# One step of a search or of its places behind a piece of the experts' products, and a later first penalty

## The chip, the cores and the metric

The kernel runs on one core of one Trainium2 chip. Its engines are TensorE (PE, with PEld for its weight loads), VectorE (DVE), ScalarE (ACT), GpSimd (POOL) and SyncE (SP, which only issues transfers here). The metric is the device's time for one execution, in microseconds: the median of several runs.

## What is computed

Two parts, one behind the other. The first is a convolution along the sequence by way of a Fourier transform; the second sends each of its 19968 rows to one of eight experts.

```python
X = np.fft.rfft(x, axis=1)                      # x: 8 x 2496 x 256
y = np.fft.irfft(X * (filt_r + 1j * filt_i), n=2496, axis=1)
...
logits = x @ w_gate                             # x = y as 19968 x 256, eight experts
order = np.argsort(-logits.flatten())
for idx in order:                               # greedy, best logit first
    tok, e = idx // E, idx % E
    if assigned[tok] >= 0 or counts[e] >= cap:  # cap = 19968 / 8 = 2496
        continue
    assigned[tok] = e
    counts[e] += 1
...
for e in range(E):                              # w1: 8 x 256 x 1024, w2: 8 x 1024 x 256
    out[assigned == e] = np.maximum(x[assigned == e] @ w1[e], 0) @ w2[e]
```

So every expert gets exactly 2496 rows, and who gets which is settled by a greedy pass over all logits.

## The kernel before

The first 420 us are the transform, its inverse, the logits (`lg`, 117 x 176 x 8) and the first search. The rows go to `xs` in device memory.

The greedy pass is done without a sort. It falls into eight phases; each finds, by a search, the threshold at which the next expert fills up, and which expert that is (`Route.phase`). A search has eleven rounds (`threshold`). In a round VectorE compares the best logit of each token with up to nine thresholds (`Gm`, L587); TensorE multiplies the mask with the one-hot experts `A` (eleven short matmuls, L595); VectorE folds the counts (`t`, `D`, `X`, L603 to L605); TensorE sums them over the partitions (L608); and VectorE takes the next three bits of the threshold (L632 to L628). After the rounds a block of VectorE's work assigns the tokens (L702 to L749), a penalty of -3e38 is put on the full expert's logits (L755 on VectorE in phase 0, eight ACTIVATEs of L757 on ScalarE in the others), and the next phase begins with a new maximum (`M`, L672), the best expert (`tmp`, `ar`) and `A` (L682).

`places` turns a phase's result into row numbers in five chunks: a one-hot row `OH` on VectorE (L788, L789), four short matmuls (L795), a sum of signs on ScalarE (L800), and then `xid` (L803, which rows of `xs` to gather) and `oid` (where to scatter). `s.last` is the instruction that writes the first chunk's `xid`; `issue_after(x)` lets an instruction stand on its engine's queue only behind x.

The experts' stage (`Ffn.run`) goes through eight experts, each with four groups of 512 rows and one of 448. The rows are gathered by GpSimd (L853) and transposed on TensorE (`turn`, L867); ScalarE and VectorE write the transposed rows as a high and a low part (`xo`, `z`, L871). The first product has eight blocks f of six matmuls into `pz` (L888). ScalarE writes the relu's high part `hl` (L894), and VectorE its low part (L902); while a search counts and no weights are to be split (`busy`), three odd blocks of the three middle groups have it done by ScalarE and GpSimd instead (`hr`, L897 and L898). The second product has 16 matmuls for each tile of 128 rows into `py` (L946, L948), which ScalarE and GpSimd evict and scatter (L958 to L960). The last half tile is L938. An expert's weights are split into high and low parts by ScalarE and VectorE (L846, L847). `pz` and the transposes share four PSUM buffers, `py` has two, and so have the search's products (`rt`).

The order on TensorE is the order of the code. `Ffn.run` yields behind every piece of a product (three matmuls of the first, four or so of the second) what it counts, 0.65, or 0.57 in the group of 448 rows. `Pump.feed` adds it to a clock and emits what is due: one step of the places (`side`) and the search's next steps (`main`). A step sets its own due time by a table of lags. A search's steps are held until the expert in front of it begins; `until` forces steps out when a gather needs their row numbers. The other engines' order is set by the build's scheduler, from the order of the code, the dependencies and its own estimate of the times.

Of the kernel before, what the change touches and what calls it, by code (L numbers as in the profile page):

```python
# [9 lines left out]
AF, OP, AX = mybir.ActivationFunctionType, mybir.AluOpType, mybir.AxisListType  # L10
# [6 lines left out]
S = B * G  # L17
# [3 lines left out]

LAGS = [(1.6, 1.2), (1.9, 1.2), (2.4, 1.4), (2.2, 1.3), (2.2, 1.2), (2.6, 1.2), (2.6, 1.2), (2.6, 1.2)]
LO, M0, M1, M7 = (4.2, 2.0, 2.2), 3.5, 4.9, 6.9
TU0, TU, PACE = 1.1, 1.15, 5
ORD, TF = (1, 0, 0, 1), (3, 5)
ORD2 = [(0, f) for f in range(6)] + [(1, f) for f in range(4)] + [(0, 6), (0, 7)] + [(1, f) for f in range(4, 8)]
I1, EZ = 5, 0.8
# [93 lines left out]
class Fft:  # L121


    def __init__(s, tc, i, xs, zd, lg, pp):
        s.tc, s.nc, s.i, s.xs, s.zr, s.lg, s.pp = tc, tc.nc, i, xs, zd, lg, pp
        s.zd = [zd[2*K1*b:2*K1*(b+1)] for b in range(B)]
        s.zw = s.zo = s.y7 = s.y9 = s.ly = None
        s.xos = []
        s.nstore = 0
        s.nz, s.st_x = 3, tc.nc.scalar  # L130
        s.cps = tc.nc.vector.tensor_copy, tc.nc.scalar.copy
        s.Y1, s.yt, s.yd, s.z, s.xr, s.vs = {}, {}, {}, {}, {}, {}
# [355 lines left out]
class Route:  # L488
# [176 lines left out]
    def phase(s, ph):  # L665

        nc = s.nc
# [29 lines left out]
        if ph < 7:  # L697
# [22 lines left out]
            with s.tc.issue_after(x.ins):  # L720
                expert()
                nc.vector.tensor_tensor_scan(cum, s.one[:117], eqm, 0.0, op0=OP.mult, op1=OP.add)
                pen = v("pen", [128, 8])
# [28 lines left out]
        if ph == 7:  # L752
            return
        if ph == 0:
            nc.vector.tensor_tensor(s.lg, s.lg, pen[:117].unsqueeze(1).to_broadcast([117, S, 8]), op=OP.add)  # L755
        for e in range(8 if ph else 0):
            nc.scalar.activation(s.lg[:, :, e], s.lg[:, :, e], AF.Identity, bias=pen[:117, e:e+1], scale=1.0)  # L757
        with s.tc.issue_after(s.last):
# [346 lines left out]
class Pump:  # L1105
# [3 lines left out]
    def __init__(s, R):  # L1109
        s.R, s.ph, s.tags, s.out, s.limit, s.clock = R, 0, set(), {}, 0, 0.0  # L1110
        s.main, s.due, s.held = R.phase(0), 0.0, False
        s.side = []
        s.on_w, s.kind = None, ''
        s.lag = dict(d=lambda t: t, G=lambda n: LAGS[s.ph][0] + 0.17 * n, X=lambda n: LAGS[s.ph][1], m=lambda t: 1.0 + 1.2*t, w=lambda t: t,
                     o=lambda t: t, p=lambda t: t, g=lambda t: 3.0)
# [38 lines left out]

    def feed(s, c):
        s.clock += c
        for u in s.side[:1]:
            if u[0] <= s.clock:
                s.step_side(u)
        while s.due <= s.clock and not s.first() and s.step_main():  # L1160
            pass

    def until(s, tag):
        while tag not in s.tags:
# [24 lines left out]
```

## Time and profile before

| | |
|---|---|
| median of three runs | 1426.28 us (1420.32 to 1427.12) |
| the profiled execution's own time | 1427.79 us |
| its span, first to last instruction | 1426.0 us |
| mean granted clock of TensorE | 0.987 |
| busy: TensorE, VectorE, ScalarE, GpSimd | 1375.7, 938.6, 715.8, 656.2 us |
| DMA, mean over the span | 107 GB/s |

An engine's busy time is a sum over stages with different limits. Matmuls are pipelined: each is shown for about 0.4 us, while the next begins 0.23 us behind it, so a busy TensorE is not one at its peak. What a change is worth is read from the waits of the engine that bounds the stage, and from what ended them. A wait's releaser is inferred; where the engine named had long been done, it was another, often a DMA.

### The profile page before, as it was taken

The numbers are of one execution on the slowest core, as the hardware profiler recorded it, in microseconds if no ns is written. First come the engines' busy times: TensorE is split into PE (matmuls) and PEld (weight loads), VectorE is DVE, ScalarE is ACT, GpSimd is POOL, SyncE is SP. The second block draws the span as 40 slices with busy tenths as digits, with TensorE's granted clock in tenths as the row PEclk, the third lists the DMA queues.
The fourth block names the chain that finished last, engine by engine and source line by source line (L and its number), as shares of the span: only waits on it lengthen the run. The fifth ranks groups of instructions, "written<-read, shape, count | busy, mean of one in ns | idle before, by whom it ended". The sixth has DMA issues, their size and how long they took to land.

```text
span 1426.0 us, 24833 instructions
## 1 busy us (share of the span) xinstructions
PE 1375.7 (96%) x9139; PEld 1142.4 (80%) x9139; DVE 938.6 (66%) x2575; ACT 715.8 (50%) x1644; POOL 656.2 (46%) x724
## 2 busy tenths in 40 slices
PE   8999999998988999999999999999999999999998
PEld 7999998776547788877887877787788788888887
DVE  6776766584686797668668768877867845333231
ACT  6777776444553464354436435534533645433332
POOL 6344443241025556554554653646536454445423
PEclk9999999998989999999999999999999999999999
DMA  9455556878961122121112112112101321111100
GB/s 357 152 166 159 159 154 174 245 266 272 345 253 56 33 96 62 32 85 49 51 36 90 54 45 84 52 43 95 45 27 54 131 71 47 41 47 54 40 23 28
DMA packets 55389, 152.37 MB, mean 107 GB/s; under 512 B 9356, under 2 KB 29964, under 8 KB 51172
## 3 DMA queue, kind: packets, MB, share of 16 engines
q0 software_dynamic: 17552, 57.72, 12.3%
q1 hardware_dynamic: 11357, 53.88, 10.4%
q10 hardware_dynamic: 26359, 39.19, 9.2%
q8 instruction: 72, 1.18, 0.3%
q14 instruction: 49, 0.40, 0.1%
HBM read 87.08 MB, written 63.70 MB: 106 GB/s over the span
## 4 chain that ended last, share of the span: by engine, by line
PE 58%; DVE 7%; ACT 2%; issue 2%; DMA 0%; POOL 0%; POOLq 0%; DVEq 0%; ACTq 0%
PE pz L888 26%; PE py L946 18%; PE py L948 9%; PE ptr L867 2%; PE rt L595 2%; DVE hl L902 1%; ACT lg L757 1%; PE py L938 1%; PE rt L795 1%; DVE OH L789 1%; DVE Gm L587 1%; ACT junka L800 1%; DVE X L605 0%; DVE z L871 0%; DMA xg<-xs,xid 0%
## 5 line engine op out<-in xcount | busy, mean ns | idle before, releaser
L946 PE MATMUL py<-w,hl 128*128 128x512 f32 x1216 | 336.4, 397 | 3.1 <-ACT y L958 3.1
L894 ACT ACTIVATE hl<-pz 128x512 fp32r<-128x512 f32 (+1 forms) x320 | 187.7, 588 | 222.2 <-PE pz L888 193.0
L959 POOL TENSOR_TENSOR y<-y 128x256 f32<-128x256 f32 x152 | 128.9, 850 | 309.0 <-ACT y L958 308.1
L888 PE MATMUL pz<-xo,w0h 128*128 128x512 f32 (+1 forms) x640 | 259.6, 406 | 8.7 <-DVE z L871 3.2
L888 PE MATMUL pz<-xo,w0l 128*128 128x512 f32 (+1 forms) x640 | 254.9, 398 | 0.0
L902 DVE SCALAR_TENSOR_TENSOR hl<-pz,hl 128x512 fp32r<-128x512 f32 x233 | 159.1, 686 | 123.0 <-ACT hl L894 110.3
L946 PEld LDWEIGHTS py<-w,hl 128*128 128x128 f32 x1216 | 210.3, 189 | 31.3 <-ACT y L958 3.5
L853 POOL DMA_INDIRECT xg<-xs,xid x160 | 167.0, 1044 | 107.3 <-issue 35.7
L958 ACT COPY y<-py 128x512 f32<-128x512 f32 x152 | 88.7, 586 | 248.3 <-PE py L948 178.2
L948 PEld LDWEIGHTS py<-w,hl 128*128 128x128 f32 x1216 | 185.6, 188 | 24.7 <-DVE hl L902 0.7
L948 PE MATMUL py<-w,hl 128*128 128x256 f32 x1216 | 200.1, 284 | 0.3 <-DVE hl L902 0.2
L888 PE MATMUL pz<-z,w0h 128*128 128x512 f32 (+1 forms) x640 | 196.6, 388 | 0.0
L960 POOL DMA_INDIRECT out<-y,oid x160 | 171.4, 1071 | 45.5 <-POOL y L959 34.7
L888 PEld LDWEIGHTS pz<-xo,w0h 128*128 128x128 f32 x640 | 121.8, 190 | 32.0 <-DVE z L871 3.9
L888 PEld LDWEIGHTS pz<-z,w0h 128*128 128x128 f32 x640 | 121.4, 190 | 21.7 <-DVE z L871 0.2
L219 ACT COPY Y<-p 64x240 f32<-64x240 f32 (+1 forms) x304 | 116.2, 382 | 41.6 <-PE p L212 20.3
L888 PEld LDWEIGHTS pz<-xo,w0l 128*128 128x128 f32 x640 | 122.3, 191 | 15.5
L235 POOL TENSOR_TENSOR P<-P 128x256 f32<-128x256 f32 x80 | 58.7, 734 | 163.2 <-DVE P L233 162.1
L587 DVE TENSOR_TENSOR Gm<-M,thr 117x1232 bf16<-117x1232 f32 (+2 forms) x80 | 104.4, 1315 | 0.2
L212 PE MATMUL p<-cS,xr 117*128 117x120 f32 x688 | 97.5, 281 | 2.3 <-DMA xr<-xl 2.3
L212 PEld LDWEIGHTS p<-cS,xr 117*128 117x128 f32 x688 | 89.3, 198 | 5.3 <-DMA xr<-xl 2.5
L227 PE MATMUL p<-cW,Y 128*128 128x128 f32 x640 | 88.1, 277 | 1.8 <-ACT Y L219 1.8
(233 smaller groups left out, 2228.7 us busy)
## 6 DMA issues: line engine op xcount, KB each, us to landing
zd<-zt ACTq DMA_DIRECT2D x80, 256.0 KB
xr<-xl SPq DMA_DIRECT2D x6, 1536.0 KB
z<-zd SPq DMA_DIRECT2D x14, 640.0 KB
xr<-xl SPq DMA_DIRECT2D x7, 1216.0 KB
xs<-xo ACTq DMA_DIRECT2D x13, 600.0 KB
xr<-zd SPq DMA_DIRECT2D x8, 640.0 KB
xs<-xr ACTq DMA_DIRECT2D x8, 600.0 KB
xs<-Y ACTq DMA_DIRECT2D x6, 600.0 KB
```

The costliest lines, as they stand in the source:

```text
L212: nc.tensor.matmul(p[:, q-q0, :120], s.xr[b][:117, q], s.cS1, start=True, stop=True)
L219: x = (nc.vector.tensor_copy if dve else nc.scalar.copy)(dst, src)
L587: nc.vector.tensor_tensor(Gm[:, s0:s1, :m], s.M[:, s0:s1].unsqueeze(2).to_broadcast([117, s1 - s0, m]), thr[:117].unsqueeze(1).to_broadcas ...
L853: s.lastg = s.nc.gpsimd.indirect_dma_start(out=xg[:n], out_offset=None, in_=s.xs, in_offset=bass.IndirectOffsetOnAxis(ap=ids[0][:n, t:t+1] ...
L888: nc.tensor.matmul(p[:, :n], w[:, sl], x[:, k, :n], start=m == 0, stop=m == 5)
L894: s.lasta = nc.scalar.activation(h[:, :n], p[:, :n], AF.Relu).ins
L902: nc.vector.scalar_tensor_tensor(l[:, :n], p[:, :n], 0.0, h[:, :n].bitcast(F32), op0=OP.max, op1=OP.subtract)
L946: nc.tensor.matmul(pp, hs[g][f][:, hi], w2[:, :, 256*f:256*f+256], start=m == 0, stop=False, skip_group_check=True)
L948: nc.tensor.matmul(pp[:, f % 2], hs[g][f][:, lo], w2h[:, 256*f:256*f+256], start=False, stop=m > 13, skip_group_check=True)
L958: s.lasta = nc.scalar.copy(yy, pp).ins
L959: nc.gpsimd.tensor_tensor(y, y, yy[:, 1], op=OP.add)
L960: st = nc.gpsimd.indirect_dma_start(out=out_rows, out_offset=bass.IndirectOffsetOnAxis(ap=ids[1][:w, 4*g+t:4*g+t+1], axis=0), in_=y[:w], i ...
```

## The change

There are two edits. In phase 0 the penalty on VectorE may stand on the queue only behind the first chunk's row numbers (`s.last`). And `Pump` gets a time `free`: from phase 1 on, a step that was emitted sets it 0.6 ahead of the clock, `feed` emits nothing before it, and it ends after one step, of the places first, else of the search.

```diff
--- before.py
+++ after.py
@@ -21,7 +21,7 @@
 
 LAGS = [(1.6, 1.2), (1.9, 1.2), (2.4, 1.4), (2.2, 1.3), (2.2, 1.2), (2.6, 1.2), (2.6, 1.2), (2.6, 1.2)]
 LO, M0, M1, M7 = (4.2, 2.0, 2.2), 3.5, 4.9, 6.9
-TU0, TU, PACE = 1.1, 1.15, 5
+TU0, TU, PACE, GAP = 1.1, 1.15, 5, 0.6
 ORD, TF = (1, 0, 0, 1), (3, 5)
 ORD2 = [(0, f) for f in range(6)] + [(1, f) for f in range(4)] + [(0, 6), (0, 7)] + [(1, f) for f in range(4, 8)]
 I1, EZ = 5, 0.8
@@ -752,7 +752,8 @@
         if ph == 7:
             return
         if ph == 0:
-            nc.vector.tensor_tensor(s.lg, s.lg, pen[:117].unsqueeze(1).to_broadcast([117, S, 8]), op=OP.add)
+            with s.tc.issue_after(s.last):
+                nc.vector.tensor_tensor(s.lg, s.lg, pen[:117].unsqueeze(1).to_broadcast([117, S, 8]), op=OP.add)
         for e in range(8 if ph else 0):
             nc.scalar.activation(s.lg[:, :, e], s.lg[:, :, e], AF.Identity, bias=pen[:117, e:e+1], scale=1.0)
         with s.tc.issue_after(s.last):
@@ -1109,7 +1110,7 @@
     def __init__(s, R):
         s.R, s.ph, s.tags, s.out, s.limit, s.clock = R, 0, set(), {}, 0, 0.0
         s.main, s.due, s.held = R.phase(0), 0.0, False
-        s.side = []
+        s.side, s.free = [], 0.0
         s.on_w, s.kind = None, ''
         s.lag = dict(d=lambda t: t, G=lambda n: LAGS[s.ph][0] + 0.17 * n, X=lambda n: LAGS[s.ph][1], m=lambda t: 1.0 + 1.2*t, w=lambda t: t,
                      o=lambda t: t, p=lambda t: t, g=lambda t: 3.0)
@@ -1154,11 +1155,18 @@
 
     def feed(s, c):
         s.clock += c
+        if s.clock < s.free:
+            return
         for u in s.side[:1]:
             if u[0] <= s.clock:
                 s.step_side(u)
+                s.free = s.clock + (GAP if s.ph else 0)
+                if s.free > s.clock:
+                    return
         while s.due <= s.clock and not s.first() and s.step_main():
-            pass
+            s.free = s.clock + (GAP if s.ph else 0)
+            if s.free > s.clock:
+                return
 
     def until(s, tag):
         while tag not in s.tags:
```

The changed program's line numbers are one higher from L755 on, and eight higher behind `feed`. Three places show what moves.

VectorE at the end of phase 0, before: the penalty `pen` of the full expert, the weights' row numbers `widx`, the penalty's addition, and the start of the chain that leads to the row numbers (`pf`: the counts of earlier partitions).

```order
L724 TENSOR_SCALAR pen<-ev 128x8
L696 SCALAR_TENSOR_TENSOR widx<-eid,row 128x1
L755 TENSOR_TENSOR lg<-lg,pen 117x1408
L736 COPY pf<-rt 117x2
L738 TENSOR_TENSOR pf<-need,pf 117x1
```

And now, behind the chain's end: the addition stands between the first chunk's `xid`, with its by-products, and the maximum's preparations.

```order
L804 SCALAR_TENSOR_TENSOR xid<-ex,js 128x4
L807 TENSOR_TENSOR t_5022<-js,row 128x28
L810 TENSOR_TENSOR t_5025<-js,ex 128x4
L756 TENSOR_TENSOR lg<-lg,pen 117x1408
L761 SCALAR_TENSOR_TENSOR asg<-m_4933,asg 117x176
L809 TENSOR_REDUCE t1b<-t_5022 128x4
```

The addition (L755, now L756) comes two dozen rows later, behind the row numbers, and the chain to them begins with no long instruction ahead of it.

VectorE at the first expert's start, before: `z` is the low part of the transposed rows, `w` a split of the second weights, `ar` and `A` the best expert of each token and its one-hot form, which phase 1's first counts multiply.

```order
L871 TENSOR_TENSOR z<-ptr,xo 128x2x256
L679 SCALAR_TENSOR_TENSOR ar<-asg,ar 117x176
L871 TENSOR_TENSOR z<-ptr,xo 128x2x256
L802 TENSOR_SCALAR js<-js 128x4
L847 TENSOR_TENSOR w_5016<-wr_5013,w_5016 128x512
L682 TENSOR_TENSOR A<-ar,row 117x1232
L847 TENSOR_TENSOR w_5016<-wr_5013,w_5016 128x512
L803 SCALAR_TENSOR_TENSOR xid<-ex,js 128x4
```

And now, from behind both `z`, `tmp` (L676) and `js`, on to `A`:

```order
L660 SCALAR_TENSOR_TENSOR ru<-rl,row,ru 128x8
L848 TENSOR_TENSOR w_5016<-wr_5013,w_5016 128x512
L678 TENSOR_REDUCE ar<-tmp 117x176
L804 SCALAR_TENSOR_TENSOR xid<-ex,js 128x4
L807 TENSOR_TENSOR t_5022<-js,row 128x28
L810 TENSOR_TENSOR t_5167<-js,ex 128x4
L848 TENSOR_TENSOR w_5016<-wr_5013,w_5016 128x512 x3
L903 SCALAR_TENSOR_TENSOR hl<-pz,hl 128x512
L679 SCALAR_TENSOR_TENSOR ar<-asg,ar 117x176
L809 TENSOR_REDUCE t1b<-t_5022 128x4
L903 SCALAR_TENSOR_TENSOR hl<-pz,hl 128x512
L682 TENSOR_TENSOR A<-ar,row 117x1232
```

`tmp` and the reduction `ar` stood ahead of the first `z` before; now they, four splits and two `hl` stand between `z` and `A`.

TensorE in the fourth expert's first group, before: two matmuls of the places of phase 3 (L795) and the sum of a round of phase 4's search (L608) stand behind the same three matmuls of the first product.

```order
L888 MATMUL pz<-xo,w0h 128x512
L795 LDWEIGHTS OH
L795 MATMUL rt<-tab_3588,OH 128x180
L795 LDWEIGHTS OH
L795 MATMUL rt<-tab_3588,OH 128x180
L608 LDWEIGHTS ones_3568
L608 MATMUL rt<-X_1_3571,ones_3568 128x28
L888 MATMUL pz<-xo,w0l 128x512
```

And now, at the nearest like place, the search's sum comes a piece, three matmuls, behind the places' pair.

```order
L796 LDWEIGHTS OH
L796 MATMUL rt<-tab_3588,OH 128x180
L796 LDWEIGHTS OH
L796 MATMUL rt<-tab_3588,OH 128x180
L889 MATMUL pz<-xo,w0h 128x512
L889 MATMUL pz<-xo,w0l 128x512
L889 MATMUL pz<-xo,w0h 128x512
L608 LDWEIGHTS ones_3568
L608 MATMUL rt<-X_0_3570,ones_3568 128x28
L889 MATMUL pz<-xo,w0l 128x512
L889 MATMUL pz<-z,w0h 128x512 x2
```

The products and their number are the same; what moved are the pairs of L795 (now L796) and the steps of the search between them.

## Rows read from the trace of the kernel before

**Rows 1.** The page's busy times: engine, busy us (share of the span) xinstructions.

```profile
PE 1375.7 (96%) x9139; PEld 1142.4 (80%) x9139; DVE 938.6 (66%) x2575; ACT 715.8 (50%) x1644; POOL 656.2 (46%) x724
```

**Rows 2.** Chain that ended last, in time order: start us, us, what (half tiles alone).

```profile
684.58 1.97 PE py L938 x16
...
941.78 1.87 PE py L938 x16
...
1192.00 1.87 PE py L938 x16
...
1307.24 1.87 PE py L938 x16
```

**Rows 3.** TensorE's waits, 437 to 1190 us: who <- for whom, us, times, longest.

```profile
PE rt L608 <- DVE X L605: 5.6, 6, 1.4
PE pz L888 <- DVE z L871: 3.2, 2, 2.0
PE py L946 <- ACT y L958: 3.1, 2, 1.5
PE pz L888 <- DVE tab L746: 2.7, 1, 2.7
```

**Rows 4.** Timeline of TensorE, three waits: start us, us, instruction, shapes xcount [idle before <-releaser].

```profile
543.76 0.17 PE L608 MATMUL rt<-X,ones 128*128 128x18 f16 x1 [0.55 <-DVE t L809]
...
772.53 0.79 PE L888 MATMUL pz<-xo,w0h 128*128 128x512 f32 x1 [2.03 <-DVE z L871]
...
1031.65 0.18 PE L608 MATMUL rt<-X,ones 128*128 128x6 f16 x1 [1.40 <-DVE X L605]
```

**Rows 5.** Timeline of VectorE, 412 to 428 us.

```profile
412.17 0.89 DVE L676 TENSOR_TENSOR tmp<-tmp,val 117x1408 bf16<-117x1408 bf16 x1
...
416.25 1.61 DVE L678 TENSOR_REDUCE ar<-tmp 117x176 f32<-117x1408 bf16 x1
...
420.69 0.69 DVE L871 TENSOR_TENSOR z<-ptr,xo 128x512 fp32r<-128x512 f32 x1
...
423.60 1.44 DVE L682 TENSOR_TENSOR A<-ar,row 117x1232 bf16<-117x1232 f32 x1
...
425.80 1.29 DVE L847 TENSOR_TENSOR w<-wr,w 128x512 fp32r<-128x512 f32 x2
...
427.00 0.68 DVE L902 SCALAR_TENSOR_TENSOR hl<-pz,hl 128x512 fp32r<-128x512 f32 x1
```

**Rows 6.** Three stretches of TensorE: us, busy (xinstructions), granted clock, DMA share, GB/s.

```profile
425.70:427.40 1.70, 1.69 (x9) 1.00 0.00 0
431.00:434.40 3.40, 3.40 (x9) 0.50 0.24 77
772.50:775.70 3.20, 3.17 (x8) 0.50 0.14 41
```

**Rows 7.** Timeline of VectorE, 395 to 407 us.

```profile
395.98 1.62 DVE L755 TENSOR_TENSOR lg<-lg,pen 117x1408 f32<-117x1408 f32 x1
...
405.82 0.16 DVE L803 SCALAR_TENSOR_TENSOR xid<-ex,js 128x4 int32<-128x4 f32 x1
```

**Rows 8.** Timeline of GpSimd, 408 to 412 us.

```profile
411.59 1.00 POOL L853 DMA_INDIRECT xg<-xs,xid  x1 [4.95 <-DVE r L774]
```

**Rows 9.** Timeline of SP's queue, 380 to 430 us.

```profile
393.57 12.29 SPq L412 DMA_DIRECT2D xs<-xo  x7
```

**Rows 10.** Timeline of TensorE, 425 to 432 us.

```profile
425.09 0.72 PE L595 MATMUL rt<-A,Gm 117*48 117x112 bf16 x11 [0.22 <-DVE A L682]
...
429.06 0.19 PE L608 MATMUL rt<-X,ones 128*128 128x21 f16 x1 [1.66 <-DVE X L605]
...
431.29 0.78 PE L888 MATMUL pz<-xo,w0h 128*128 128x512 f32 x1
```

**Rows 11.** GpSimd's group of subtractions: xcount | busy us, mean ns | idle before <-releasers.

```profile
L898 POOL TENSOR_TENSOR hl<-hr,hl 128x512 fp32r<-128x512 f32 x23 | 31.5, 1371 | 6.6 <-ACT hr L897 5.6 <-ACT hl L894 0.6
```

**Rows 12.** Timeline of VectorE, 1029 to 1032 us.

```profile
1029.65 1.95 DVE L605 TENSOR_TENSOR X<-D,row 48x6 f16<-48x6 f32 x1
```


## The prediction, made before the changed kernel was run

> **What bounds the kernel now.** I read the page's busy times first: TensorE is busy for 96% of the span [rows 1], so time can only come from the 50 us in which it stands, or from rows in which it runs slowly. Then the chain that ended last, for the length of one expert. Between the half tiles at 684.58 and 941.78 lie two experts with a search beside them, 128.6 us each; between 1192.00 and 1307.24 lies one without, 115.2 us [rows 2]. The 13.4 us more are the search's own matmuls, which the change keeps, and the waits that it causes. Third, TensorE's waits from 437 to 1190 us: the four largest rows [rows 3] come to 14.6 us, ten smaller ones to 7.9, together 22.5. All but 5 us of it ends on VectorE, and none of it on a DMA. So the experts' stage is bound by TensorE, and what can be won there is VectorE being late: 22.5 us at most. The stage before the experts ends with a wait for the gather, which is read apart below.
>
> **What the change moves.** Run through the emission, the kernel before puts its 328 steps of search and places behind 294 pieces of the products; 34 pieces carry two, nearly always one of each kind. In the changed one, 327 pieces carry steps and one carries two (forced by the first expert's third gather, as before). But a piece counts 0.65 and the gap is 0.6: the next piece is barred only where it counts 0.57, in an expert's last block. There were 7 steps at that distance and now there are none; steps one full piece apart rise from 38 to 59. So the first half of the change is done everywhere, the second hardly. Beyond the first expert no step is forced out by a gather that needs it, before or after; the seventh expert's first row numbers are emitted 24 units (some 37 pieces) later than before and still 27 units ahead of their gather, so lateness costs nothing.
>
> **Two steps behind one piece.** I took the 34 places and looked for waits of TensorE in the 9 us behind each: 13 waits, from 0.55 us at 543.76 to 1.40 us at 1031.65, the largest 2.03 at 772.53 [rows 4], 11.0 us together. At 1031.65 a places step and a counting step share one piece: on VectorE the one-hot row is made between the arrival of the counts and their first use. The other 11.5 us of the 22.5 stand behind single steps (the long blocks that end a search, the penalties on ScalarE), and those only change place. A step moved by one piece, 0.7 us, still comes to the same VectorE, and a mask or a maximum there takes 1.44 or 1.61 us [rows 5]; so I do not take the whole 11.0. Ends: 11.0 gained, and 5 lost, if the new places are as unlucky as the two waits of 2.0 and 2.7 (the z of 772.53 [rows 4] and the row that names L746 [rows 3]). I take half, -5.5. After 772.53 the granted clock is 0.50 (1.2 GHz of 2.4) for 3.2 us with 8 instructions, where 9 take 1.7 us at 1.00 [rows 6]: some 1.6 us lost, of which half again, -0.8.
>
> **The first penalty.** It takes 1.62 us on VectorE and stands ahead of the chain that ends in the first row numbers at 405.82 [rows 7]. That chain could gain 1.6. But the gather that reads the numbers starts only at 411.59 [rows 8], 5.6 us after they are written. The row names an instruction of VectorE that it does not need; what is left for it are the stores of the rows that it gathers, which SP issues until 405.9 [rows 9]. So the gain is 0, with -1.6 as the far end.
>
> **What the move pushes back.** Behind the row numbers the penalty delays the maximum and all that follows it, and the order changes with it: the vector of experts A, which the first search's counts need, stood directly behind the second z and one split. Now the maximum's last parts, four splits and two hl stand between them (second piece of the order). Worked out from [rows 5], from z's end at 421.4: 0.89 + 1.61 + four splits (0.65 each, 2.6) + two hl (1.36) + seven small ones of 0.16 to 0.33 (1.4) + 1.44 for A gives 430.7, where before A ended at 425.04. TensorE reaches these counts at 424.9 in either program, because nothing ahead of it moves; it would stand 5.8 us instead of 0.22 [rows 10]. Behind the counts in its queue are the third group of products, the second product of the search and the transposes of the next rows. But before, it stood there too: 1.66 us for X at 429.06, then for the gather, and the next products began at 431.29 [rows 10], at half clock until 434.4 [rows 6]. After: counts to 431.4, six matmuls at half clock 2.5, transposes 0.6, so these products begin at 434.5, 3.2 late. They then run at full clock, 1.4 instead of 2.6, which leaves 2.0 late; and where the search's next counts waited too, a part is taken up, by estimate 0.8. I take +1.2. Ends: 0, if hl comes earlier than I think, and +6.8, if nothing behind it waits any more (5.6 and the 1.2 of half clock).
>
> **GpSimd's subtractions.** The relu's remainder goes to GpSimd while the search counts and no split is open. The search is stretched, so there are 33 of these for 23, each 1.37 us there and 0.68 less on VectorE [rows 5, 11]. At 1029.65 the small X, which takes 0.2 elsewhere, took 1.95 and ended with such a subtraction [rows 12]; the wait of 1.40 at 1031.65 is its end. Three such waits among 23 subtractions make at most 10 x 3/23 x 1.40 = +1.8; VectorE's 6.8 us of relief, off the path, take back some. I take +0.9.
>
> The Trainium skill speaks against this term as I size it. GPSIMD Engine Reference, Specifications, says that GpSimd's interfaces to SBUF are shared with VectorE, and contended by VectorE instructions with two SBUF inputs, which X is. The row at 1029.65 agrees. By the rule each added subtraction can hold one; the sum by it is the last rival.
>
> **Sum.** -5.5 - 0.8 + 0 + 1.2 + 0.9 = -4.2. The profiled execution took 1427.79, so 1423.6 by its own time. It lies 1.5 above the median of the runs, 1426.28, which gives **1422.1**, said as 1422.
>
> **Rivals.**
> - *More is won*, 1414. All 13 waits go and the half clock with them (-12.6), the rest of the sum is as above (+2.1), and a fifth of the 11.5 behind single steps goes too (-2.3): -12.8. For it: 19 of the 34 doubles sit in a search's beginning, where VectorE has its longest instructions. Against it: VectorE's total work there is the same, and the steps one piece apart have risen by 21.
> - *The burst is only moved*, 1427. VectorE still gets both steps within 1.4 us; the waits fall elsewhere in the same number: 0 + 1.2 + 0.9 less a little = about +1. For it: half of the waits stand behind single steps; and the gap bars next to nothing beyond the one piece.
> - *The first counts wait for A uncovered*, 1434. TensorE's queue stops at the counts at 424.9 until A is written, and no later wait shrinks: +6.8, with the +0.9 and no gain from the spread +7.7. It decides if A ends after 430 and the products behind 431.29 are late by more than 5 us. Against it: the gather and X held TensorE there until 431 anyway.
> - *Every added subtraction holds an X*, 1435. Ten more waits of 1.40 are +14, with -6.3 from the spread and +1.2 at the first counts +8.9. For it: X's end at 1031.60 beside the subtraction's. Against it: 20 of 23 subtractions met no wait. (This is the rule of the Trainium skill's GPSIMD Engine Reference, taken at its full.)
>
> **How the numbers follow.** Forecast 0.50 (1417 to 1427), more won 0.19, only moved 0.17, first counts 0.10, subtractions 0.04. Half a per cent is 7 us, about what a measurement of this kernel can tell from no change (its three runs lie 6.8 apart). Faster by that (under 1419): 0.12 of the forecast's 0.50 and nearly all of "more won", 0.31. Slower by that (over 1433.4): most of the last two, 0.11. The rest, 0.58. For 8 in 10 the range reaches to the middle of "more won" and to the first counts' rival: 1411 to 1432; the likeliest case alone has 1417 to 1427.
>
> **What would show it.** Right, step by step: the gather's start stays within 0.5 us of 411.6; TensorE waits 4 to 6 us for A at the first counts, and the half clock falls there; the wait for the gather behind it is gone; the waits of TensorE from 437 to 1190 come to 15 to 18 us, with X, z and hl smaller and the penalties' rows (y) as before; GpSimd has 33 subtractions. Wrong: those waits at 22 or more (then the double pieces were not the cause), the experts' length at 128 or above, a first product that starts over 1 us earlier (then the numbers, not the stores, held the gather), or the products behind the first gathers over 4 us late.

## The result, and the profile after

The changed kernel took 1410.9 us (median of 6 runs, 1409.0 to 1413.9), the kernel before 1427.9 (median of 6, 1420.3 to 1433.4) beside it. The ratio is 0.9898, with an interval of 0.9876 to 0.9920: 1.0% faster (the two medians alone would give 0.988). The forecast was 1422 in a range from 1411 to 1432, so the time lies at the very low end of the range. In the profiled executions 18.0 us are gone (1427.79 to 1409.78; spans 1426.0 and 1408.0). They lie here (an expert is counted from the last half-tile matmul of the one in front of it, the first expert from the first product):

| part | before, us | after, us | difference |
|---|---|---|---|
| to the first product | 419.9 | 415.0 | -4.8 |
| first expert | 138.2 | 140.1 | +1.9 |
| second to sixth expert | 635.6 | 619.8 | -15.7 |
| seventh and eighth | 227.3 | 227.7 | +0.4 |

The page's busy times of after (engine, us, share, instructions): TensorE is busy for 7 us less than in [rows 1] with the same 9139 matmuls, and it stands 39 us instead of 50.

```profile
PE 1368.8 (97%) x9139; PEld 1139.1 (81%) x9139; DVE 944.6 (67%) x2565; ACT 719.8 (51%) x1654; POOL 679.2 (48%) x734
```

**The first 4.8 us are no part of the change.** Up to the moved penalty (395.98 in before, [rows 7]) TensorE and VectorE have the same instructions in the same order. The timeline of TensorE has the first matmul of the transform's second stage here, in before and in after (start us, us, engine line op, tiles, shapes):

```profile
35.47 0.36 PE L291 MATMUL pa<-yh,cEh 128*128 128x256 f32 x1
```

```profile
31.14 0.36 PE L291 MATMUL pa<-yh,cEh 128*128 128x256 f32 x1
```

So 4.3 of the 4.8 were there by 35 us. The windows of the first transforms (stretch, us, busy time and instructions of TensorE, its weight loads, VectorE, ScalarE and GpSimd, granted clock, DMA share, GB/s) show why, before and after:

```profile
6.00:8.00 2.00, 0.00 (x0) 0.00 (x0) 1.15 (x4) 1.91 (x7) 2.00 (x4) 0.93 0.98 369
...
7.80:14.50 6.70, 6.44 (x30) 6.44 (x31) 3.05 (x8) 2.12 (x6) 6.70 (x14) 0.50 1.03 421
```

```profile
6.00:8.00 2.00, 1.16 (x10) 1.16 (x11) 1.06 (x4) 1.92 (x7) 2.00 (x4) 1.00 1.02 410
8.00:10.00 2.00, 2.00 (x20) 2.00 (x20) 1.90 (x5) 1.37 (x4) 2.00 (x5) 1.00 1.06 429
```

In before TensorE waited 2.3 us for a load, and then ran at half clock until 14.5. In the twelve profiles below the same matmul starts at 30.9 to 34.0; the profile of before is the latest of fourteen. In this pair of profiles the change itself is worth the other 13 to 14 us.

**The waits in the experts.** TensorE's waits from 437 to 1190 us, all of after, for [rows 3] (who <- for whom, us, times, longest):

```profile
PE rt L608 <- DVE X L605: 2.6, 3, 1.3
PE pz L889 <- DVE dr L774: 1.9, 1, 1.9
PE pz L889 <- DVE hl L906: 1.0, 1, 1.0
PE rt L608 <- DVE t1b L809: 0.8, 1, 0.8
PE pz L889 <- DVE z L872: 0.8, 1, 0.8
PE pz L889 <- DVE t L810: 0.7, 1, 0.7
PE pz L889 <- DVE hl L903: 0.5, 1, 0.5
PE ptr L868 <- DVE hl L903: 0.4, 1, 0.4
PE py L947 <- ACT y L959: 0.3, 1, 0.3
PE pz L889 <- issue: 0.2, 1, 0.2
PE pz L889 <- DVE xid L804: 0.2, 1, 0.2
```

They come to 9.4 us instead of 22.5. The search's own matmuls (`rt`) wait 3.4, where seven rows of before, from X with 5.6 down to 0.3, come to 9.8. The chain of waits has the half tiles, for [rows 2]:

```profile
553.48 1.90 PE py L939 x16
676.45 1.87 PE py L939 x16
802.17 1.87 PE py L939 x16
...
1052.27 1.87 PE py L939 x16
```

From 553.48 to 802.17 the second and the third expert took 124.3 us each. In before these two had 128.1, and the third and fourth of [rows 2] 128.6.

**Where the penalty waits went.** The two rows y and tab of [rows 3] are 5.8 us, and both have one cause, the penalty that ends a search: eight instructions on ScalarE (L757, L758 after). Before, at the end of the sixth search, on ScalarE, and then VectorE and TensorE (start us, us, instruction, [idle before <-releaser]):

```profile
1106.01 4.29 ACT L757 ACTIVATE lg<-lg,pen 117x176 f32<-117x176 f32 x8 [1.68 <-DVE pen L724]
1110.19 0.59 ACT L894 ACTIVATE hl<-pz 128x512 fp32r<-128x512 f32 x1
...
1110.81 0.69 DVE L902 SCALAR_TENSOR_TENSOR hl<-pz,hl 128x512 fp32r<-128x512 f32 x1 [1.83 <-ACT hl L894]
...
1111.56 0.50 PE L888 MATMUL pz<-xo,w0h 128*128 128x512 f32 x1 [2.67 <-DVE tab L746]
```

For 4.3 us ScalarE evicts no `pz`. First products stand beside it, one every 1.5 us, and the four buffers fill. The next matmul starts 0.06 us after VectorE has read the oldest one; the row names `tab` only as VectorE's next instruction. The Trainium skill (Perfetto Trace Analysis, Optimization Strategy) says that the same gap, repeated on the engine that should be busy, can mean that SBUF or PSUM has no room for the next tile. Here the want of room is the cause, but the gaps are not the same: they go from 0 to 2.67 us for six like blocks. The two waits of the row y, 1.51 and 1.54 us, stand behind such blocks too. There it is ScalarE's eviction of `py` that comes late, with two buffers; this is the later one, on ScalarE and then TensorE:

```profile
987.17 4.39 ACT L757 ACTIVATE lg<-lg,pen 117x176 f32<-117x176 f32 x8 [1.67 <-DVE pen L724]
991.47 1.04 ACT L958 COPY y<-py 128x512 f32<-128x512 f32 x2
...
992.08 1.66 PE L946 MATMUL py<-w,hl 128*128 128x512 f32 x6 [1.54 <-ACT y L958]
```

In after the same block, on ScalarE:

```profile
994.04 4.50 ACT L758 ACTIVATE lg<-lg,pen 117x176 f32<-117x176 f32 x8 [0.28 <-DVE pen L724]
...
1118.83 4.42 ACT L758 ACTIVATE lg<-lg,pen 117x176 f32<-117x176 f32 x8
```

It is as long as before. But the one at 1118.83 has the end of one first product beside it and then second products, and TensorE never waits; the one at 994.04 costs 0.26. Before, the six blocks cost 0, 1.51, 0, 0, 1.54 and 2.67 us.

**The start of the experts.** SP's stores, VectorE's first row numbers and the penalty, GpSimd's first gather, VectorE's A, and TensorE's first counts and third products, from the timelines of these engines in after, for [rows 7 to 10]:

```profile
387.91 11.74 SPq L412 DMA_DIRECT2D xs<-xo  x7
...
399.82 0.16 DVE L804 SCALAR_TENSOR_TENSOR xid<-ex,js 128x4 int32<-128x4 f32 x1
...
400.07 1.62 DVE L756 TENSOR_TENSOR lg<-lg,pen 117x1408 f32<-117x1408 f32 x1
...
405.93 1.48 POOL L854 DMA_INDIRECT xg<-xs,xid  x1 [5.31 <-DMA xs<-xo]
...
424.07 1.44 DVE L682 TENSOR_TENSOR A<-ar,row 117x1232 bf16<-117x1232 f32 x1
...
425.57 1.22 PE L595 MATMUL rt<-A,Gm 117*48 117x112 bf16 x11 [5.07 <-DVE A L682]
...
430.29 0.61 PE L889 MATMUL pz<-xo,w0h 128*128 128x512 f32 x1
```

The gather stands 6.1 us behind its row numbers (5.8 before) and now names the stores. TensorE waits 5.07 us for A. From the first product to the third ones it takes 15.3 us (430.29 - 415.04) instead of 11.4.

### The profile page after: what moved, and what is told of

It reads as the page before. It is cut to its first block, busy times and chain, and to the rows that moved or that the text cites. A ratio compares the mean times of both kernels' runs of the same rounds, so it can differ in the third digit from the quotient of the medians.

```text
span 1408.0 us, 24843 instructions
## 1 busy us (share of the span) xinstructions
PE 1368.8 (97%) x9139; PEld 1139.1 (81%) x9139; DVE 944.6 (67%) x2565; ACT 719.8 (51%) x1654; POOL 679.2 (48%) x734
## 3 DMA queue, kind: packets, MB, share of 16 engines
q8 instruction: 72, 1.18, 0.3%
## 4 chain that ended last, share of the span: by engine, by line
PE 84%; DVE 6%; DMA 2%; ACT 2%; issue 1%; POOL 1%; ACTq 0%; POOLq 0%; DVEq 0%
PE pz L889 28%; PE py L947 19%; PE py L949 10%; PE pv L408 5%; PE p L227 4%; PE p L212 4%; PE pa L291 4%; PE rt L595 2%; PE ptr L868 2%; PE pa L246 2%; PE pv L257 1%; DMA zd<-zt 1%; PE rt L796 1%; PE py L939 1%; DVE Gm L587 1%
## 5 line engine op out<-in xcount | busy, mean ns | idle before, releaser
L960 POOL TENSOR_TENSOR y<-y 128x256 f32<-128x256 f32 x152 | 119.9, 790 | 250.7 <-ACT y L959 249.2
L854 POOL DMA_INDIRECT xg<-xs,xid x160 | 172.5, 1078 | 126.8 <-issue 31.5
L903 DVE SCALAR_TENSOR_TENSOR hl<-pz,hl 128x512 fp32r<-128x512 f32 x223 | 152.4, 687 | 95.3 <-ACT hl L895 86.5
L961 POOL DMA_INDIRECT out<-y,oid x160 | 177.2, 1108 | 48.1 <-POOL y L960 34.3
L889 PEld LDWEIGHTS pz<-xo,w0l 128*128 128x128 f32 x640 | 122.2, 191 | 15.7
L212 PE MATMUL p<-cS,xr 117*128 117x120 f32 x688 | 94.4, 274 | 1.3 <-DMA xr<-xl 1.3
L212 PEld LDWEIGHTS p<-cS,xr 117*128 117x128 f32 x688 | 86.2, 191 | 4.2 <-issue 2.5
```

The lines of the kernel that those rows point to most:

```text
L212: nc.tensor.matmul(p[:, q-q0, :120], s.xr[b][:117, q], s.cS1, start=True, stop=True)
L854: s.lastg = s.nc.gpsimd.indirect_dma_start(out=xg[:n], out_offset=None, in_=s.xs, in_offset=bass.IndirectOffsetOnAxis(ap=ids[0][:n, t:t+1] ...
L889: nc.tensor.matmul(p[:, :n], w[:, sl], x[:, k, :n], start=m == 0, stop=m == 5)
L903: nc.vector.scalar_tensor_tensor(l[:, :n], p[:, :n], 0.0, h[:, :n].bitcast(F32), op0=OP.max, op1=OP.subtract)
L960: nc.gpsimd.tensor_tensor(y, y, yy[:, 1], op=OP.add)
L961: st = nc.gpsimd.indirect_dma_start(out=out_rows, out_offset=bass.IndirectOffsetOnAxis(ap=ids[1][:w, 4*g+t:4*g+t+1], axis=0), in_=y[:w], i ...
```

## The experiments

Sums are from each kernel's profile; the ratio is to runs of the kernel before beside it on the same chip. Between kernels whose steps are fed alike (changed and 1, before and 2) the sum of the second to the sixth expert differs by 0.9 and 1.1 us, so no difference of 1 us is read from it. "Behind blocks" are TensorE's waits of over 0.1 us from 1 us after the start of each penalty block on ScalarE to 2.5 us after its last instruction's start. The pieces with two steps are counted by the pump's clock (the prediction counted 34 for the kernel before).

| kernel | double pieces | experts 2-6, us | all eight, us | waits 437-1190 | behind blocks | ratio (95%) |
|---|---|---|---|---|---|---|
| before | 33 | 635.6 | 1001.0 | 22.5 | 5.7 | 1 |
| changed | 1 | 619.8 | 987.6 | 9.4 | 0.3 | 0.990 (0.988-0.992) |
| 1 spreading alone | 1 | 618.9 | 985.9 | 9.4 | 0.3 | 0.990 (0.987-0.992) |
| 2 penalty alone | 33 | 634.5 | 1002.3 | 19.1 | 5.7 | 1.002 (1.001-1.003) |
| 3 gap 0.7 | 9 | 667.0 | 1041.4 | 37.1 | 1.2 | 1.031 (1.028-1.033) |
| 4 changed, no GpSimd subtraction | 1 | 618.8 | 985.3 | 8.4 | 0.2 | 0.990 (0.987-0.992) |
| 5 bunched | 65 | 632.2 | 1001.2 | 18.4 | 6.2 | 0.999 (0.998-1.000) |
| 6 spread, lags -0.15 | 1 | 623.8 | 990.7 | 12.3 | 3.7 | 0.991 (0.990-0.992) |
| 7 lags +0.20 | 30 | 630.0 | 995.7 | 15.9 | 6.8 | 0.996 (0.994-0.997) |
| 8 spreading, no GpSimd subtraction | 1 | 617.7 | 982.4 | 7.5 | 0.2 | 0.985 (0.984-0.987) |
| 9 lags +0.15 | 34 | 618.9 | 988.9 | 11.8 | 1.0 | 0.990 (0.988-0.992) |
| 10 lags +0.10 | 35 | 625.9 | 991.5 | 15.7 | 4.1 | 0.994 (0.991-0.996) |
| 11 lags -0.10 | 31 | 625.9 | 990.7 | 14.4 | 3.9 | 0.994 (0.992-0.996) |
| 12 as 8, lags +0.10 | 1 | 623.9 | 988.7 | 12.1 | 0.0 | 0.991 (0.990-0.993) |

**1 and 2: each edit alone.** The first has `feed` as changed and the first penalty without its `issue_after`; the second the reverse.

> The spreading alone, with the first penalty back ahead of the first row numbers. Theory: the spreading shortened the second to the fifth expert (128.2, 128.0, 129.1, 128.8 us before; 123.0, 125.7, 122.9, 127.3 after) and the moved penalty lengthened the first (138.2 to 140.1) through the late vector A; so here the first expert takes 138 again, the others 123 to 127 as after, about 1409 us, 2 below the changed kernel. Rival (the moved penalty earns something itself): slower than the changed kernel, 1414 or more, with the gather's start later against the last matmuls of the transform. On the transform: its first matmuls waited 2.3 us for a load and ran at half clock before, 1.3 us and full clock after, 4.4 us in all; if that is chance, it falls either way here.

> The moved penalty alone, the steps fed as in the kernel before. Theory: the first expert 140 us instead of 138.2, the second to the fifth 128 to 129 as before, 1428 to 1431 us. Rival (the moved penalty brings the gain, by another draw of all later positions): the second to the fifth expert at 123 to 127 and the time near 1415. On the transform: with its start at full clock the profile's first product stands near 415, else near 420; if the edit caused it, it is 415 here in every run.

The spreading carries all of the gain, 1407.0 us. The moved penalty alone is 1426.6 beside 1423.5, slower by 0.2%. The first expert did not quite fall to 138 without it (139.3); with it alone it is 140.5. Over all the runs here its length goes from 137 to 142 us, so these differences show little. The gather gains nothing in either: 6.3 us behind its row numbers with the penalty ahead of them (398.39, 404.72), 7.3 with it behind (398.69, 405.98). In both profiles TensorE starts early (31.7 and 30.9 at L291), the second without any spreading, so that this was chance.

**3: a gap that bars the next piece.**

```
-TU0, TU, PACE, GAP = 1.1, 1.15, 5, 0.6
+TU0, TU, PACE, GAP = 1.1, 1.15, 5, 0.7
```

> The gap at 0.7 instead of 0.6, so that the next full piece of 0.65 is really barred: steps one full piece apart fall from 59 to 12, those two pieces apart rise; the search beside an expert is longer by 5 to 9 units and 18 steps of the places come only when a gather asks for them. Theory (VectorE is late because steps come close together): TensorE's waits from 437 to 1190 us fall below the 10 us of the changed kernel, to 5 or 6, and the time to 1406 to 1409. Rival (the gain is one draw of positions among many): periods of the experts scatter between 123 and 129 us again, 1411 to 1425. Rival (the forced steps are late): waits for the gather of 1 to 3 us each, slower than the changed kernel, 1414 to 1420.

3.1% slower, 1468.0 us; the rival of the forced steps was right in kind and far too small. TensorE's waits, the largest (437 to 1190 us):

```profile
PE ptr L868 <- DMA xg<-xs,xid: 21.1, 12, 4.7
PE pz L889 <- DVE z L872: 4.1, 4, 1.6
PE py L949 <- POOL hl L899: 4.1, 2, 2.4
```

The row numbers come when the gather asks for them, and the transposes wait for the rows. In none of the other profiles from 437 us on is the gather a row.

**4: no subtraction on GpSimd.**

```
-                    W.busy = lambda: pump.kind in 'GX' and not split
+                    W.busy = lambda: False
```

> The changed kernel with all of the relu's remainders on VectorE, none on GpSimd (33 before this edit), the steps unmoved. Theory (the spreading is what counts): VectorE has 0.68 us more in 33 places, which it has time for; experts 0 to 1 us longer each, 1411 to 1416 us. Rival (the ten more subtractions on GpSimd, which the longer search brings, are what relieved VectorE): the second to the fifth expert go back to 127 to 129 us, 1422 to 1428. Rival (each subtraction on GpSimd holds an X): faster than the changed kernel, 1405 to 1409.

1408.4 us, the same ratio as the changed kernel, and 1.0 us less in the second to the sixth expert. So the ten more subtractions are not what relieved VectorE. What all 33 together cost is about 1 us there, no more than the scatter, and 2.3 us over all eight experts. By the rule that the prediction took from the Trainium skill's GPSIMD Engine Reference, Specifications, each could hold a VectorE instruction with two SBUF inputs. The traces here show some that held X: its longest from 425 us on is 1.95 us in before and 1.52 in after, and 0.75 without subtractions. They show nearly none that held TensorE: its waits for X are 2.6 us with 33 subtractions and 2.3 with none.

**5: more double pieces, everything else in its place.**

```
-            if u[0] <= s.clock:
+            if u[0] <= s.clock and (not s.ph or s.first() or s.main is None or s.held or s.due <= s.clock or s.clock - u[0] > 1.3):
```

> The kernel before, with more double pieces and nothing else: a step of the places that is due waits up to 1.3 units for a step of the search and then shares its piece. 65 pieces carry two steps instead of 33; the search itself stays where it is and as long as before, and GpSimd has the same 23 subtractions. Theory (two steps behind one piece are what makes VectorE late): the waits from 437 to 1190 us rise from 22.5 to 33 or more, and the second to the sixth expert, 635.6 us together before and 619.8 with the spreading, take 645 to 655; 1433 to 1443 us. Rival (any redraw of positions moves the time by some us either way): 1415 to 1430. Rival (only the length of the search counts): no change, 1423.

This is the run on which my theory fell. Twice the double pieces cost nothing in it: 1422.5 beside 1423.3, and fewer waits than before. The waits (437 to 1190 us):

```profile
PE pz L888 <- DVE z L871: 3.7, 4, 2.0
PE py L946 <- ACT y L958: 3.6, 2, 2.1
PE rt L608 <- DVE X L605: 2.6, 3, 1.4
PE pz L888 <- DVE tab L746: 2.6, 1, 2.6
PE ptr L867 <- DVE hl L902: 2.5, 3, 1.9
```

X fell to 2.6 as in the changed kernel, though twice as many counting steps share a piece. The y and tab waits stayed, and the penalty blocks stand in the same products as before (the last wait is 2.63 at 1107.76): the search had not moved.

**6 and 7: the length of the search and the spreading apart from each other.** In `Pump`, lags of G and X less 0.15 with the spreading of the first experiment, and plus 0.20 with the feed of the kernel before:

```
-... G=lambda n: LAGS[s.ph][0] + 0.17 * n, X=lambda n: LAGS[s.ph][1], ...
+... G=lambda n: LAGS[s.ph][0] + 0.17 * n - (0.15 if s.ph else 0), X=lambda n: LAGS[s.ph][1] - (0.15 if s.ph else 0), ...
```

> One step per piece as in the first experiment (penalty undone), and the lags of the search shortened by 0.15 units from the second expert's search on, so that the searches end where they do in the kernel before (636 units instead of 631; 658 in the changed kernel) and GpSimd has 23 subtractions as before. Theory: the gain comes from one step per piece, so it stays, 1405 to 1410 us, the second to the sixth expert 618 to 624 us together. Rival (the gain came from the longer search, that gives VectorE more time for each answer): the gain is gone, 630 us or more for these experts, 1418 to 1425.

> The kernel before with the lags of the search 0.2 units longer from the second expert's search on: the searches end later than in the changed kernel (676 units, 658 there, 631 before), but 30 pieces still carry two steps, and GpSimd has 39 subtractions. Theory (two steps behind one piece): the waits stay at 18 to 24 us and the time at 1418 to 1428. Rival (a longer search does it): waits of 10 or less and 1405 to 1412.

1411.6 and 1417.3 us. Both lie between the ranges of the two theories, 1.6 and 0.7 us from that of the double pieces: spread and short keeps most of the gain, double and long gets 6 us of it. So the length alone is not the cause; that the spreading alone is not either, the fifth and the ninth experiment show.

**8: the two faster variants together.**

> The two edits that were each at least as fast as the changed kernel, together: the spreading without the moved penalty, and no subtraction on GpSimd. The first was at 1407.0, the second at 1408.4, the changed kernel at 1410.9. If both add up, 1404 to 1406; if the two only removed the same waits of the first expert, 1407 to 1409.

1403.6 us, the fastest: ratio 0.9854 (0.9840 to 0.9868), whose interval lies just under that of the changed kernel. It lies just below what was expected if both add up.

**9 to 11: the search moved by its lags alone**, with the feed and the penalty of the kernel before (`+ 0.15`, `+ 0.10` and `- 0.10` as in the diff of 6).

> The kernel before with the lags of the search 0.15 units longer, which brings the ends of the second to the fifth search (146.7, 246.1, 345.1, 443.9 units) to where they are in the changed kernel (141.6, 246.1, 348.8, 445.2; before 139.7, 239.8, 337.9, 429.6), while 34 pieces still carry two steps. The theory of the double pieces fell with the fifth experiment, so two are left. Theory now (where the long blocks of VectorE and ScalarE that end a search fall in the expert decides): as good as the changed kernel, the second to the sixth expert at 618 to 624 us together, 1407 to 1412 us. Rival (steps that stand apart are better wherever they are, if they move the search's counting steps away from the places): 629 to 636 us, 1418 to 1424.

> The kernel before with lags 0.10 units longer: the second and third search end where they do before (139.7, 239.8), the others 1 to 14 units later (338.6, 437.4, 537.5, 631.7), 35 double pieces. Theory (the place of the long blocks decides): the second and third expert as before, 128 us each, the fourth to the sixth shorter than before by 2 to 5 us each; 1415 to 1420. Rival (steps apart): all as before, 1421 to 1426.

> The kernel before with lags 0.10 units shorter: searches end at 139.7, 232.0, 324.9, 415.9, 508.2, 601.2 units, farther from the changed kernel, 31 double pieces. Theory (the place of the long blocks decides): no order to expect beyond a new draw, 625 to 645 us for the second to the sixth expert. Rival (steps apart, the double pieces being as many): 632 to 638 us, as before. Rival (a longer search is better by itself): slower than before, 638 or more, 1427 or more.

The ninth gives the whole gain with 34 double pieces: 1411.2 us, 618.9 for the second to the sixth expert. It is the one that decides against the spreading: the gain can be had without it, by moving the search near to where the changed kernel has it. But the two agree in their sum alone. The second to the sixth expert take 126.9, 125.2, 123.9, 120.9 and 122.0 us here, and 122.9, 125.7, 122.9, 127.2 and 121.0 in the changed kernel, so that the same place gives the same time is not shown. The tenth, at 1414.4, came just under the 1415 to 1420 that the theory gave. The fourth and fifth expert are shorter by 3.4 us each, as it said; the sixth is not, and the second and third, at 126.7 and 126.2, were shorter than its 128, though the second and third search end where they did before. The eleventh is faster too (1414.6) with a shorter search, so a longer one is not better by itself. All three moves beat the place that the kernel before has.

**12: the fastest, with its search moved.** Experiment 8 with lags longer by 0.10.

> The fastest so far (spreading alone, no subtraction on GpSimd) with lags 0.10 units longer: the searches end at 141.6, 246.8, 349.5, 451.5, 551.6, 648.6 units, up to 8 later than there. Theory (the place of the long blocks decides): the second and third expert as in the eighth experiment, 123 and 125 us, the fourth to the sixth another draw, 120 to 128 each. Rival (steps apart): all stay within 1 us of the eighth experiment's, 617 to 620 together, 1403 to 1405 us.

1411.6 us: 6.2 more for the second to the sixth expert than in 8 with the same spreading, of which 4.1 in the second, where the theory had said none. No wait stands behind a penalty block, and still the waits are 12.1, the largest of them these (437 to 1190 us):

```profile
PE ptr L867 <- DVE hl L902: 3.3, 4, 1.1
PE pz L888 <- DVE z L871: 3.3, 5, 1.2
PE pz L888 <- DVE xid L803: 2.3, 1, 2.3
```

The last stands behind two long instructions of VectorE that begin a phase (`tmp` 1.42 and `ar` 1.61 us), most of the others behind one-hot rows and splits of 0.3 to 0.8 us. So the penalty blocks are one part of what the place decides, not all; and the place of a search's end alone does not forecast an expert's length.

## Why the prediction was right in its sign and short in its size

- **The start.** The gather bound by the stores was right: its row names them now, and the numbers' place moved nothing. "A first product over 1 us earlier" would have proved this wrong by my own sign; it came 4.8 earlier, but with the matmuls of the first 35 us, so the sign was badly chosen: it should have been the gather's distance from the stores.
- **A late.** Right: a wait of 5.07 (5.8 worked out) at the first counts, no wait for the gather behind it, the third products 3.8 later against the first (3.2 worked out), and the half clock there (0.50 from 423.8 to 430.5). The whole was expected at +1.2; the runs give +0.2% or 2.8 us for the penalty alone, and +1.9 for the first expert in the profile. Which part of my sum was too small is not shown.
- **Two steps behind one piece, -5.5.** This is the step that failed, in its cause and so in its size. I credited the 13 waits that stand behind double pieces, and said that the other half of the waits "only change place". Experiment 5 shows twice as many double pieces that cost nothing; experiment 9 that moving the search without undoing them is worth the same. What moved is the place of the search against the products, and there the kernel before has the worst of the places tried, apart from the gap of 0.7. The waits came to 9.4 us, not to the 15 to 18 that I gave. Of the 13.1 us that went, 5.4 are the penalty blocks, which I forecast to stay "as before", and 6.4 are the search's own matmuls, whose waits fell in the bunched kernel as well (3.8 of 9.8 left). Why these wait less in both is not shown. That the time still fell within the range was luck as far as this term goes.
- **The half clock.** One stretch went (772.53), another came. Behind a wait of 1.85 us at 1013.64 the window of after shows it, with 10 instructions in 3.3 us (9 took 1.7 at 1.00, [rows 6]):

```profile
1014.30:1017.60 3.30, 3.30 (x10) 2.54 (x9) 3.30 (x5) 0.60 (x1) 0.99 (x2) 0.50 0.28 88
```

  That wait is the kind that is left. On VectorE the `z` of the next rows stands behind a maximum (M) of the new phase and a split (start us, us, instruction):

```profile
1010.70 1.61 DVE L672 TENSOR_REDUCE M<-lg 117x176 f32<-117x1408 f32 x1
1012.23 0.68 DVE L848 TENSOR_TENSOR w0l<-wr,w0h 128x512 fp32r<-128x512 f32 x1
1012.83 0.15 DVE L774 TENSOR_TENSOR dr<-dr,ge 128x8 f32<-128x8 f32 x1
1012.91 0.68 DVE L872 TENSOR_TENSOR z<-ptr,xo 128x512 fp32r<-128x512 f32 x1
```

- **GpSimd's subtractions, +0.9.** 33 as forecast. All of them cost 1.0 us in the second to the sixth expert and 2.3 in all eight (experiment 4; 1.2 and 3.5 between 1 and 8), so by estimate ten cost 0.3 to 1.1: the size fits. The way of it, waits for X, does not, as these are 2.6 us with the subtractions and 2.3 without.
- **The rivals.** "More is won" had the time nearly right at 1414, with the same wrong cause. "The burst is only moved" was right that doubles do not matter, and wrong that the waits would come to the same number. I had the waits of one place of the search, that of the kernel before, and took their number as usual.

What stays open: what it is in a place that makes the waits many or few, beyond the penalty blocks, and whether one step per piece has a worth of its own. With the lags unchanged it is ahead by 13.4 us over the eight experts, but its search stands elsewhere. With the lags longer by 0.10 it is a little ahead of double pieces (988.7 and 991.5 us, and there GpSimd's subtractions are gone as well), but the best kernel moved by its lags alone (988.9) lies among the spread ones (982.4 to 990.7). Nor was the penalty block cut into shorter pieces, which would test its 5.4 us by themselves.

## What to carry to other kernels

Where a side task's long blocks run beside a pipeline with few buffers, ask of each block which products stand beside it and how many buffers these have, before you ask how many steps share a place. And before a rule of order is credited with a gain, move the old order by a little in both directions: if that gains as well, the old place was bad, and the rule is one way among several to leave it. And look whether the rule delays something else: here the gap of 0.7 starved a gather, and its 21.1 us of waits were nearly the 22.5 of all the waits before.

## What the hardware showed

- One wait for a load in the first 8 us cost 4.3 us in the profile of before: 1.0 more of waiting, and the rest in the 6.7 us at half clock. The same instructions reached L291 anywhere between 30.9 and 35.5 us.
- With eight instructions of 0.55 us in a row ScalarE stopped TensorE for 0 to 2.7 us, by the products that stood beside them; for an engine that is busy for 50% of the span that was a quarter of the waits.
- GpSimd's subtractions took 1371 ns on the mean in before [rows 11] and 1586 in after, but not by their number: experiment 6 had 23 of them at 1547, experiment 3 had 50 at 1472. In after (xcount | busy us, mean ns | idle before):

```profile
L899 POOL TENSOR_TENSOR hl<-hr,hl 128x512 fp32r<-128x512 f32 x33 | 52.3, 1586 | 16.2 <-ACT hr L898 15.6
```

- An X takes 0.2 us as a rule. In every kernel with these subtractions one from 425 us on took 1.18 us or more, up to 2.0; in the three kernels without them (4, 8 and 12) none took over 0.8.
